# Attention pairs in plain float32: quotients by column halves, one exponential for 512 columns, a reordered weight conversion

## The chip, the cores and the metric

One Trainium2 chip, and of it one core. A core has TensorE (matrix products, PE in the profile, with its weight loads as PEld), VectorE (DVE), ScalarE (ACT), GpSimd (POOL) and SyncE (SP), which issues most DMAs here. Each engine works through its own list of instructions in order and waits on semaphores. The metric is the device time of one execution in microseconds, as the median of several runs.

## The reference

Three stages in a row, all in float32. The attention has 4 batches of 8 heads, 576 positions and 64 columns per head; `omega` is 128 x 64.

```python
def phi(x):                                   # x: q or k, scaled by D ** -0.25
    proj = np.einsum('bhsd,md->bhsm', x, omega)
    h = proj - np.sum(x * x, axis=-1, keepdims=True) / 2.0
    h = h - np.max(h, axis=-1, keepdims=True)
    return np.exp(h) / np.sqrt(m)
kv = np.einsum('bhsm,bhsd->bhmd', k_p, v)
z = np.sum(k_p, axis=2)
num = np.einsum('bhsm,bhmd->bhsd', q_p, kv)
den = np.einsum('bhsm,bhm->bhs', q_p, z)[..., None] + 1e-06
attn = num / den
```

Its result, as 2304 rows of 512 columns, goes through two MLPs with a hidden width of 2048: `h = x @ w_in`, then `max(h, 0) + alpha * min(h, 0)` in the first and 0, `(h + 1) ** 2 / 4` or `h` by ranges in the second, then `g @ w_out`.

## The kernel before

**The attention** goes by pairs of heads: 16 pairs, four for each batch. For a pair, `features` multiplies `omega` with the keys (and later the queries) of both heads, four blocks of 128 positions each, into one PSUM bank per head; `last_features` does the remaining 64 positions. `exponentials` takes each row's maximum on VectorE (`nm`) and then the exponential on ScalarE, one instruction for each block of 128 columns, because the maximum enters as a bias that holds for one block alone. `key_sums` gives `kv` and `z` (a column of ones beside `v`); its copies out of PSUM are `kv_hi`. `transposed` turns the query features (`qh`). `quotients` multiplies `qh` with `kv` and `z`, for half of the positions and one head at a time, into 64 rows of numerators and 64 rows of denominators of one bank; VectorE turns the denominators (`den`), ScalarE or VectorE copies the numerators (`num`). `back` inverts `den` and lets GpSimd multiply both into `x`, the input of the first MLP.

The first six pairs (`N_FULL`) use plain float32 products. The later pairs, and both MLPs, use three products of a faster kind with operands split in two, a rounded part (`_hi`) and the rest (`_lo`): `mm3`. Splitting costs a ScalarE copy and a subtraction, on VectorE for `x`, `g` and the queries, on GpSimd for weights.

**The weights** arrive as float64 bit patterns (`raw`). `convert` makes float32 of each 128 x 512 tile: two scalings (ScalarE, the first one sometimes on GpSimd), a shift and a sign step on VectorE, an addition on GpSimd. Sixteen weight blocks (`f`) of each MLP have two such tiles.

**The MLPs** go by units: for one MLP, one group of positions and one weight block, `hidden` computes `h` from `x` (12 products of 512 columns for a batch), `activate` makes `g`, and `project` adds to four banks `y` (12 more products). The groups are batches 0, 1, 2, and 3 with the left-over positions. So the first unit needs pairs 0 to 3, and pairs 4 to 15 run between the units of the first MLP. The products of unit i+1's `h` stand ahead of unit i's `y`, so that `activate` has time.

**The order** on each engine is written out by a planner in Python (class `Plan`). Work is a set of streams that yield steps with an engine and an assumed duration; the planner repeatedly emits the step that can start first, by rank where several can. Where a step names two engines it takes the one that would end first. The ranks (`attention_rank`, `weight_rank`) say how far ahead of the units attention and weights go. Tokens stand for buffers: `k_slot`, `q_slot`, `l_slot` for the features, `split_slot` for a pair that has not yet all its exponentials, `free_banks` for PSUM banks. The assumed durations are in `_act`, `_dve`, `_pool`, `_dma` and constants as `KV_NS`.

Of the kernel before, what the change touches and what calls it, by code (L numbers as in the profile page):

```python
# [8 lines left out]
F32 = mybir.dt.float32  # L9
# [147 lines left out]
def _dma(nbytes, emit):  # L157
    return "dma", 60 + nbytes / 200, emit
# [3 lines left out]
def favor_attention_two_mlps(  # L162
# [20 lines left out]
    nc = tc.nc  # L183
# [17 lines left out]
    WARM = 18  # L201
    ROWS_NS = 298
# [18 lines left out]
    def attention_rank(pair):  # L221
        b, hp = divmod(pair, NP)
        return hp - 8 if b == 0 else NF * (b - 1) + NF // NP * (hp + 1)
# [43 lines left out]
    def convert(dst, src, key):  # L267

        n = dst.shape[1]
        yield raws  # L270
        raw = stage_p.tile([P, 2 * n], U32, tag="raw", name="raw", bufs=RAWS)
        yield _dma(P * n * 8, lambda: nc.sync.dma_start(raw, src))
        f = raw.bitcast(F32).rearrange("p (n t) -> p n t", t=2)[:, :, 1]
        h = raw.bitcast(U16).rearrange("p (n t) -> p n t", t=4)[:, :, 1]
        low, e = (raw.rearrange("p (n t) -> p n t", t=2)[:, :, t] for t in range(2))
        d = dst.bitcast(U32)

        yield [
            _act(n, lambda: nc.scalar.activation(f, f, AF.Copy, scale=2.0**-112)),
            _pool_one(n, lambda: nc.gpsimd.tensor_scalar(f, f, 2.0**-112, 0.0, ALU.mult, ALU.add), 300),  # L280
        ]
        yield _act(n, lambda: nc.scalar.activation(low, h, AF.Copy, scale=2.0**-13))
        yield _dve_fast(n, lambda: nc.vector.tensor_scalar(d, e, 3, None, ALU.logical_shift_left))  # L283
        yield _pool(n, lambda: nc.gpsimd.tensor_tensor(d, d, low, ALU.add))  # L284
        yield _dve_two(
            n,
            lambda: nc.vector.scalar_tensor_tensor(
                d, e, 0x80000000, d, ALU.bitwise_and, ALU.bitwise_or
            ),
        )  # L290
        plan.put(raws, 0)
        done("w", *key)
# [44 lines left out]
    k_slot, q_slot, l_slot, t_slot, den_slot = (Tokens([0]) for _ in range(5))  # L337
# [9 lines left out]
    def exponentials(pool, pr, tag, dst, key):  # L347
# [6 lines left out]
        yield _dve(n * M, lambda: nc.vector.tensor_reduce(nm, pv, AX.X, ALU.max, negate=True))  # L354
        for i in range(n):
            yield _act(
                M, lambda: nc.scalar.activation(dst[:, i, :], pv[:, i, :], AF.Exp, bias=nm[:, i : i + 1]), 40  # L357
            )
# [3 lines left out]
    def features(pool, x, t0, f, keys, needs, r):  # L362
# [10 lines left out]
        def products():  # L373
            for t in range(NJ):
                c = slice((t0 + t) * P, (t0 + t + 1) * P)
                for h in range(2):
                    rows = slice(h * D, (h + 1) * D)
                    o = prs[h][:, t * M : (t + 1) * M]
                    nc.tensor.matmul(o, x[rows, c], om[rows, h * M : (h + 1) * M], start=True, stop=True)  # L379
# [5 lines left out]
    def last_features(pool, x, lf, key, needs):  # L385
# [5 lines left out]
            432, lambda: nc.tensor.matmul(o, x[:, 2 * NJ * P : 2 * NJ * P + P], om, start=True, stop=True)  # L391
# [3 lines left out]
    def key_sums(pool, kf, lf, vm, vl, pair):  # L395
# [38 lines left out]

        def his():
            for h in range(2):
                o = kv_hi[:, h, cs[h]]
                nc.scalar.activation(o.bitcast(F32) if one else o, kv3[:, h, :D], AF.Copy)
            nc.scalar.activation(z_hi.bitcast(F32) if one else z_hi, z, AF.Copy)
# [7 lines left out]
        yield "act", 370, his  # L447
        if not one:
            yield "dve", 472, los
# [38 lines left out]
    def quotients(kv_hi, kv_lo, qh, ql, den, num, i, h, pair):  # L488
# [3 lines left out]
        if pair < N_FULL:  # L492
            a, b = kv_hi[:, h, :].bitcast(F32), qh[:, h, c].bitcast(F32)
            yield _pe(490, lambda: nc.tensor.matmul(n[:, :SH], a, b, start=True, stop=True))
        else:
            yield _pe(
                mm3_ns(SH),
                lambda: mm3(n[:, :SH], kv_hi[:, h, :], kv_lo[:, h, :], qh[:, h, c], ql[:, h, c], True, True),
            )
        done("n", pair, i, h)  # L500
        own, other = (slice(0, D), slice(D, 2 * D))[:: 1 - 2 * h]

        yield "dve", 508, lambda: nc.vector.transpose(den[own, c], n[other, :SH])
        yield [
            _act(SH, lambda: nc.scalar.copy(num[own, c], n[own, :SH]), 0),
            _dve(SH, lambda: nc.vector.tensor_copy(num[own, c], n[own, :SH]), 50),
        ]
        give(tag)
        done("den", pair, i, h)

    def back(pool, qh, ql, b, hp, pair):
# [6 lines left out]
        num = pool.tile([P, S], F32, tag="num", name="num")  # L518
        for i in range(2):
            for h in range(2):  # L520
                plan.add(quotients(kv_hi, kv_lo, qh, ql, den, num, i, h, pair), attention_rank(pair), pair - 50)
# [55 lines left out]
    def attend(pool):  # L577
        for pair in range(B * NP):
# [3 lines left out]
            yield split_slot  # L582
# [7 lines left out]
            lf = pool.tile([P, 2, M], F32, tag="lf", name="lf")  # L590
# [14 lines left out]
            for key in ("k0", "k1", "l", "q0", "q1"):  # L605
                yield ev(key, pair)
            plan.put(split_slot, 0)
# [216 lines left out]
    om = pool.tile([P, 2 * M], F32, name="om")  # L824
    nc.vector.memset(om, 0.0)
    nc.vector.memset(half, 0.5)

    warm = const.tile([P, 1], F32, name="warm")
    nc.scalar.activation(warm, half, AF.Exp)
    warm_w = const.tile([P, 2 * M], F32R, name="warm_w")  # L830
    nc.vector.memset(warm_w.bitcast(F32), 0.0)
# [3 lines left out]
    for i in range(2):  # L835
        nc.scalar.dma_start(om[i * D : (i + 1) * D, i * M : (i + 1) * M], omega)
# [24 lines left out]
    def constants():  # L861
        make_identity(nc, ident)
        nc.scalar.activation(om, om, AF.Copy, scale=QK_SCALE)

# [65 lines left out]
```

## Time and profile before

| | |
|---|---|
| median of 3 runs | 942.61 us (942.48 to 943.08) |
| the profiled execution | 942.46 us, of which the span of the trace is 940.7 us |
| TensorE | 920.2 us busy, 98% of the span, granted clock 0.999 |
| VectorE, ScalarE, GpSimd | 549.5, 521.5 and 453.7 us busy |

Engines, lines and idle times are named in the rows below. A line number is that of the kernel before. A row of a timeline gives start, duration, engine, line, operation, output and input tiles; in brackets stands the idle time of the engine just before it and what ended it. Durations of instructions that follow each other closely overlap: what one costs its engine is the distance to the next start.

### The profile page before, as it was taken

To read this page: it belongs to the slowest core of one execution; us is meant where nothing else is said; L and a number is where in the kernel's file an instruction comes from. 1 tells how busy PE (TensorE), PEld (TensorE's weight loads), DVE (VectorE), ACT (ScalarE), POOL (GpSimd) and SP (SyncE) were. 2 spreads that over 40 slices of the span, in tenths; PEclk is the share of its full clock that TensorE was granted. 3 is DMA by queue.
4 is the path that set the end of the run, shared out by engine and by line. 5 is a ranking of instruction groups with operands and counts; after the bars stand their busy time and mean duration, and the time that the engine had idled before them with its cause. 6 is when DMAs were issued, how large, how long until landed. Compare 5 with 4: busy or idle time off the path is not lost.

```text
span 940.7 us, 14096 instructions
## 1 busy us (share of the span) xinstructions
PE 920.2 (98%) x5196; PEld 760.6 (81%) x5196; DVE 549.5 (58%) x927; ACT 521.5 (55%) x1120; POOL 453.7 (48%) x374
## 2 busy tenths in 40 slices
PE   8889999999999999999999999999999999999997
PEld 6667887788887888878888888888888888888886
DVE  4898787866667567777764443353335344533332
ACT  6989767655556645655642354464446445543343
POOL 1658776443334357766762344444444444332330
PEclk9999999999999999999999999999999999999999
DMA  7555443111121001334420000010001000100002
GB/s 209 172 157 175 150 150 128 39 38 39 39 63 65 2 1 45 114 111 135 135 91 1 1 0 1 1 45 1 0 1 45 1 1 1 45 1 1 1 1 68
DMA packets 33861, 53.41 MB, mean 57 GB/s; under 512 B 20992, under 2 KB 21120, under 8 KB 33792
## 3 DMA queue, kind: packets, MB, share of 16 engines
q1 hardware_dynamic: 33632, 52.45, 17.4%
q8 instruction: 41, 0.67, 0.3%
q14 instruction: 28, 0.23, 0.1%
q10 hardware_dynamic: 160, 0.07, 0.0%
HBM read 47.78 MB, written 4.72 MB: 56 GB/s over the span
## 4 chain that ended last, share of the span: by engine, by line
PE 89%; DVE 4%; ACT 4%; issue 1%; DMA 0%; POOL 0%; ACTq 0%
PE h L258 14%; PE h L259 14%; PE h L257 14%; PE y L257 12%; PE y L258 12%; PE y L259 12%; PE a L257 2%; PE a L379 2%; PE a L259 2%; PE a L258 2%; ACT kf L357 1%; PE a L416 1%; PE a L464 1%; ACT qf L357 1%; DVE x_lo L251 1%; DVE nm L354 1%
## 5 line engine op out<-in xcount | busy, mean ns | idle before, releaser
L252 POOL TENSOR_TENSOR w_lo<-w,w_hi 128x512 fp32r<-128x512 f32 x256 | 335.7, 1312 | 394.4 <-ACT w_hi L241 387.4
L241 ACT ACTIVATE w_hi<-w 128x512 fp32r<-128x512 f32 x256 | 161.6, 632 | 197.1 <-PE h L258 125.7
L257 PE MATMUL h<-x_hi,w_hi 128*128 128x512 f32 (+1 forms) x640 | 239.9, 375 | 0.0
L258 PE MATMUL h<-x_lo,w_hi 128*128 128x512 f32 (+1 forms) x640 | 236.2, 369 | 2.9 <-DVE x_lo L251 2.9
L259 PE MATMUL h<-x_hi,w_lo 128*128 128x512 f32 (+1 forms) x640 | 236.0, 369 | 0.2 <-POOL w_lo L252 0.2
L241 ACT ACTIVATE g_hi<-h 128x512 fp32r<-128x512 f32 (+1 forms) x160 | 88.9, 555 | 94.0 <-DVE h L679 46.5
L258 PEld LDWEIGHTS h<-x_lo,w_hi 128*128 128x128 f32 x640 | 120.7, 189 | 23.8 <-DVE x_lo L251 4.2
L257 PEld LDWEIGHTS h<-x_hi,w_hi 128*128 128x128 f32 x640 | 120.7, 189 | 21.2 <-DVE g_lo L250 0.8
L259 PEld LDWEIGHTS h<-x_hi,w_lo 128*128 128x128 f32 x640 | 120.6, 188 | 21.0 <-POOL w_lo L252 0.6
L250 DVE TENSOR_TENSOR g_lo<-h,g_hi 128x512 fp32r<-128x512 f32 (+1 forms) x160 | 100.7, 636 | 52.5 <-ACT g_hi L241 50.2
L677 DVE TENSOR_SCALAR t<-h 128x512 f32<-128x512 f32 x80 | 51.0, 638 | 131.3 <-PE h L259 129.6
L284 POOL TENSOR_TENSOR w<-w,raw 128x512 uint32<-128x512 uint32 x64 | 87.1, 1364 | 39.4 <-DVE w L283 23.2
L673 DVE TENSOR_SCALAR t<-h,alpha_sb 128x512 f32<-128x512 f32 x80 | 55.6, 694 | 85.3 <-PE h L259 83.8
L257 PE MATMUL y<-g_hi,w_hi 128*128 128x512 f32 x256 | 104.6, 408 | 0.0
L258 PE MATMUL y<-g_lo,w_hi 128*128 128x512 f32 x256 | 100.3, 392 | 0.0
L259 PE MATMUL y<-g_hi,w_lo 128*128 128x512 f32 x256 | 100.0, 391 | 0.0
L257 PE MATMUL y<-w_hi,g_hi 128*128 128x512 f32 x256 | 99.8, 390 | 0.0
L258 PE MATMUL y<-w_lo,g_hi 128*128 128x512 f32 x256 | 99.8, 390 | 0.0
L259 PE MATMUL y<-w_hi,g_lo 128*128 128x512 f32 x256 | 99.6, 389 | 0.0
L678 ACT ACTIVATE t<-t,half 128x512 f32<-128x512 f32 x80 | 54.5, 681 | 59.9 <-DVE t L677 59.9
L679 DVE TENSOR_TENSOR h<-h,t 128x512 f32<-128x512 f32 x80 | 51.5, 644 | 49.6 <-ACT t L678 49.6
L259 PEld LDWEIGHTS y<-g_hi,w_lo 128*128 128x128 f32 x256 | 48.1, 188 | 10.5
(113 smaller groups left out, 1282.0 us busy)
## 6 DMA issues: line engine op xcount, KB each, us to landing
raw<-w SPq DMA_DIRECT2D x64, 512.0 KB, 4.2
kq<-kq SPq DMA_DIRECT2D x15, 576.0 KB, 4.9
vm<-v SPq DMA_DIRECT2D x16, 256.0 KB, 3.2
out<-x SPq DMA_DIRECT2D x16, 256.0 KB, 2.0
vl<-v SPq DMA_DIRECT2D x32, 16.0 KB, 2.9
out<-x SPq DMA_DIRECT2D x4, 128.0 KB, 2.3
kq<-kq SPq DMA_DIRECT2D x1, 320.0 KB, 4.0
kq<-kq SPq DMA_DIRECT2D x1, 256.0 KB, 2.8
```

Source lines behind the costliest of these rows:

```text
L241: ops = [_act(n, lambda: nc.scalar.activation(hi, src, AF.Copy))]
L250: "dve": _dve(n, lambda: nc.vector.tensor_tensor(*args), bias),
L252: "pool": _pool(n, lambda: nc.gpsimd.tensor_tensor(*args)),
L257: nc.tensor.matmul(out_, wh, mh, start=first, stop=False)
L258: nc.tensor.matmul(out_, wh, ml, start=False, stop=False)
L259: nc.tensor.matmul(out_, wl, mh, start=False, stop=last)
L284: yield _pool(n, lambda: nc.gpsimd.tensor_tensor(d, d, low, ALU.add))
L357: M, lambda: nc.scalar.activation(dst[:, i, :], pv[:, i, :], AF.Exp, bias=nm[:, i : i + 1]), 40
L673: yield _dve(n, lambda: nc.vector.tensor_scalar(tn, hn, 0.0, a, ALU.min, ALU.mult))
L677: yield _dve(n, lambda: nc.vector.tensor_scalar(tn, hn, -1.0, 1.0, ALU.max, ALU.min))
L678: yield _act(n, lambda: nc.scalar.activation(tn, tn, AF.Square, bias=half[:, 0:1], scale=0.5), 50)
L679: yield _dve(n, lambda: nc.vector.tensor_tensor(hn, hn, tn, ALU.max))
```

## The change

It touches the float32 pairs (0 to 5), the conversion of weights and the planner's figures.

1. Quotients of float32 pairs: `full_quotients` takes two banks for half of the positions. One gets the products with `z` of both heads (64 columns of weights each, head 0 into rows 0 to 63, head 1 into rows 64 to 127), the other those with `kv`. Two transposes of 128 rows for a pair take the place of four of 64 rows, and so do two copies of `num`.
2. For the second head of a float32 pair (`k1`, `q1`), VectorE subtracts the maxima of all 512 columns on the way out of PSUM, and one ScalarE exponential takes all 512.
3. The copies of `kv` and `z` of a float32 pair are two in place of three and may go to VectorE.
4. In `convert` the sign step works on the scaled low bits and stands ahead of the shift; GpSimd's addition is last. For the first ten tiles the planner prefers GpSimd for the first scaling.
5. `split_slot` is gone, `l_slot` has two buffers. Attention of batches 1 to 3 has a rank lower by 4. The planner's DMA rate is 340 in place of 200 bytes per ns, and the assumed costs of the key-sum copies of later pairs are higher.
6. `omega` is loaded once per half on two queues (ScalarE's ahead of its table load, SyncE's first of all), 128 columns wide; `om_two` is copied from it.

```diff
-    return "dma", 60 + nbytes / 200, emit
+    return "dma", 60 + nbytes / 340, emit
...
-        return hp - 8 if b == 0 else NF * (b - 1) + NF // NP * (hp + 1)
+        return hp - 8 if b == 0 else NF * (b - 1) + NF // NP * (hp + 1) - 4
...
-            _pool_one(n, lambda: nc.gpsimd.tensor_scalar(f, f, 2.0**-112, 0.0, ALU.mult, ALU.add), 300),
+            _pool_one(n, lambda: nc.gpsimd.tensor_scalar(f, f, 2.0**-112, 0.0, ALU.mult, ALU.add), -600 if early else 300),
...
-        yield _dve_fast(n, lambda: nc.vector.tensor_scalar(d, e, 3, None, ALU.logical_shift_left))
-        yield _pool(n, lambda: nc.gpsimd.tensor_tensor(d, d, low, ALU.add))
+
         yield _dve_two(
             n,
             lambda: nc.vector.scalar_tensor_tensor(
-                d, e, 0x80000000, d, ALU.bitwise_and, ALU.bitwise_or
+                low, e, 0x80000000, low, ALU.bitwise_and, ALU.bitwise_or
             ),
         )
+        yield _dve_fast(n, lambda: nc.vector.tensor_scalar(d, e, 3, None, ALU.logical_shift_left))
+        yield _pool(n, lambda: nc.gpsimd.tensor_tensor(d, d, low, ALU.add))
...
+        if key[0] in ("k1", "q1") and key[1] < N_FULL:
+
+            most = nm.unsqueeze(2).to_broadcast([P, n, M])
+            yield _dve(n * M, lambda: nc.vector.tensor_tensor(dst, pv, most, ALU.add))
+            give(tag)
+            yield _act(n * M, lambda: nc.scalar.activation(dst, dst, AF.Exp), 10)
+            done(*key)
+            return
...
+        def his_dve():
+            kvz = kv_hi.bitcast(F32).rearrange("m a (h d) -> m a h d", h=2)
+            nc.vector.tensor_copy(kvz[:, 0], kv3[:, :, :D])
+            nc.vector.tensor_copy(kvz[:, 1], z)
...
-        yield "act", 370, his
+        yield [("act", 420, his), ("dve", 420, his_dve, -200)] if one else ("act", 590, his)
...
+    def full_quotients(kvz, qt, den, num, i, pair, r):
...
+        def products():
+            for a in (1, 0):
+                for h in range(2):
+                    o = ns[a][h * D : (h + 1) * D, :SH]
+                    nc.tensor.matmul(o, kvz[:, a, h, :], qt[:, h, c], start=True, stop=True)
+
+        yield _pe(COLS_NS, products)
+        done("n", pair, i, 0)
+        done("n", pair, i, 1)
+        plan.add(evicted(turned(den[:, c], ns[1][:, :SH]), tags[1], ("den", pair, i, 1)), *r)
+        plan.add(evicted(copied(num[:, c], ns[0][:, :SH]), tags[0], ("den", pair, i, 0)), *r)
...
-            yield split_slot
...
-            lf = pool.tile([P, 2, M], F32, tag="lf", name="lf")
+            lf = pool.tile([P, 2, M], F32, tag="lf", name="lf", bufs=2)
...
+    for queue, r in ((nc.scalar, slice(0, D)), (nc.sync, slice(D, 2 * D))):
+        queue.dma_start(om[r, :], omega)
...
-    for i in range(2):
-        nc.scalar.dma_start(om[i * D : (i + 1) * D, i * M : (i + 1) * M], omega)
```

How the order moves on TensorE around the first unit's `h`, of before (`h_544` is the first unit's hidden bank, `h_896` the second's; L494 a quotient of pair 4, L410 and L416 the key sums of pair 5):

```order
L494 MATMUL y_841<-qh,kv_hi 128x288
L257 MATMUL h_544<-x_hi,w_hi 128x512
...
L259 MATMUL h_544<-x_hi,w_lo 128x512
L494 MATMUL a_889<-qh,kv_hi 128x288
L494 MATMUL y_903<-qh,kv_hi 128x288
...
L494 MATMUL y_909<-qh,kv_hi 128x288
L410 MATMUL y_917<-vl_122,lf 64x130 x2
L416 MATMUL y_917<-vm_121,kf 64x65 x16
```

And of the change (`h_386` is the first unit's bank; L552 the new quotients of pair 4, L425 and L431 the key sums of pair 5, L489 a transpose of pair 5, L394 and L406 features of pair 6):

```order
L552 MATMUL a_855<-qh,kv_hi 64x288 x2
L425 MATMUL y_870<-vl_123,lf 64x130 x2
L431 MATMUL y_870<-vm_122,kf 64x65 x16
L491 MATMUL a_896<-ident,lf 128x128
L258 MATMUL h_386<-x_hi,w_hi 128x512
L259 MATMUL h_386<-x_lo,w_hi 128x512
L260 MATMUL h_386<-x_hi,w_lo 128x512
L489 MATMUL a_901<-ident,qf 128x128 x4
...
L406 MATMUL y_916<-om_two,kq 128x256
L258 MATMUL h_386<-x_hi,w_hi 128x512
```

All quotients of pair 4 and the key sums of pair 5 now stand ahead of the first `h`; the key and left-over features of pair 6 stand inside it, and the query features of pair 6 and the second transpose of pair 5 follow ahead of the first `y`, where before they stood after it.

On VectorE, between the split of the first input (`x_lo`) and the first step of `activate` (`t`), of before:

```order
L251 TENSOR_TENSOR x_lo<-x_127,x_hi 128x512 x4
L287 SCALAR_TENSOR_TENSOR w<-raw,w 128x512
L283 TENSOR_SCALAR w<-raw 128x512
L503 STREAM_TRANSPOSE den<-y_841 64x288
L673 TENSOR_SCALAR t<-h_544,alpha_sb 128x512
```

And of the change, from the instruction after `x_lo`:

```order
L530 STREAM_TRANSPOSE den<-a_844 128x288
L530 STREAM_TRANSPOSE den<-y_856 128x288
L288 SCALAR_TENSOR_TENSOR raw<-raw 128x512
L589 TENSOR_SCALAR inv<-den 128x18
L590 RECIPROCAL inv<-inv 128x18
L288 SCALAR_TENSOR_TENSOR raw<-raw 128x512
L594 STREAM_TRANSPOSE den<-inv 128x576
L292 TENSOR_SCALAR w<-raw 128x512
L361 TENSOR_REDUCE nm<-y_805 128x4
L361 TENSOR_REDUCE nm<-y_906 128x4
L365 TENSOR_TENSOR qf<-y_805,nm 128x4x128
L728 TENSOR_SCALAR t<-h_386,alpha_sb 128x512
```

Twelve VectorE instructions in place of four now lead from `x_lo` to the first `t`: pair 4's inversion, a query half of pair 5 and the first key maxima of pair 6 are among them.

## Rows read from the trace of the kernel before

**Rows 1.** The page, part 1: busy us, share of the span, instructions.

```profile
PE 920.2 (98%) x5196; PEld 760.6 (81%) x5196; DVE 549.5 (58%) x927; ACT 521.5 (55%) x1120; POOL 453.7 (48%) x374
```

**Rows 2.** Busy time by stretch: PE, PEld, DVE, ACT, POOL, then PEclk, DMA, GB/s.

```profile
20.00:40.00 20.00, 16.31 (x175) 11.59 (x174) 16.48 (x35) 19.85 (x67) 10.60 (x11) 1.00 0.64 201
40.00:60.00 20.00, 16.33 (x175) 12.00 (x176) 18.33 (x33) 19.29 (x58) 11.67 (x11) 1.00 0.55 166
```

**Rows 3.** Timeline of PE: key features of pairs 0, 1, 5; first `h`; first `y`.

```profile
6.46 2.08 PE L379 MATMUL y<-om,kq 64*128 64x128 f32 x16 [0.78 <-ACT om L863]
14.82 1.16 PE L379 MATMUL a<-om,kq 64*128 64x128 f32 x16
...
53.84 1.16 PE L379 MATMUL y<-om,kq 64*128 64x128 f32 x16
...
58.55 0.50 PE L258 MATMUL h<-x_lo,w_hi 128*128 128x512 f32 x1 [0.92 <-DVE x_lo L251]
...
67.00 0.39 PE L257 MATMUL y<-g_hi,w_hi 128*128 128x512 f32 x1
```

**Rows 4.** Timeline of ACT, before the first unit.

```profile
5.99 0.42 ACT L863 ACTIVATE om<-om 128x256 f32<-128x256 f32 x1 [3.76 <-DMA om<-omega]
...
33.68 0.69 ACT L241 ACTIVATE w_hi<-w 128x512 fp32r<-128x512 f32 x1
34.20 0.73 ACT L282 ACTIVATE raw<-raw 128x512 uint32<-128x512 uint16 x1
...
37.87 0.50 ACT L357 ACTIVATE kf<-y,nm 128x128 f32<-128x128 f32 x1
38.12 0.44 ACT L505 COPY num<-y 64x288 f32<-64x288 f32 x1
```

**Rows 5.** Timeline of DVE, before the first unit; then two lines of tile raw, 0:60.

```profile
28.91 1.50 DVE L503 STREAM_TRANSPOSE den<-y 64x288 f32<-64x288 f32 x3
...
40.48 0.29 DVE L480 COPY qh<-a 128x128 f32<-128x128 f32 x1
...
44.59 1.01 DVE L354 TENSOR_REDUCE nm<-y 128x4 f32<-128x512 f32 x2
...
53.26 0.78 DVE L535 STREAM_TRANSPOSE den<-inv 128x576 f32<-128x576 f32 x1
...
L283 DVE TENSOR_SCALAR w<-raw x7: 380/414/1505, 23.0 to 54.5; 128x512 uint32<-128x512 uint32 x7
L287 DVE SCALAR_TENSOR_TENSOR w<-raw,w x6: 649/685/878, 30.4 to 54.0; 128x512 uint32<-128x512 uint32 x6
```

**Rows 6.** Timeline of PE among units: key sums, then a quotient, between MLP products.

```profile
90.21 1.10 PE L416 MATMUL a<-vm,kf 128*64 128x65 f32 x32
91.24 0.50 PE L257 MATMUL y<-g_hi,w_hi 128*128 128x512 f32 x1
91.58 0.40 PE L258 MATMUL y<-g_lo,w_hi 128*128 128x512 f32 x1
91.81 0.40 PE L259 MATMUL y<-g_hi,w_lo 128*128 128x512 f32 x1
92.05 0.65 PE L494 MATMUL a<-qh,kv_hi 128*128 128x288 f32 x2
...
92.76 0.39 PE L258 MATMUL h<-x_lo,w_hi 128*128 128x512 f32 x1
```

**Rows 7.** The chain that ended last: start us, us, what (attention between units).

```profile
73.10 0.44 PE a L464 x4
74.94 1.42 PE a L379 x16
...
80.02 0.48 PE a L391 x2
...
83.92 1.09 PE a L379 x16
```

**Rows 8.** Waits of PE: line, releaser, us in total, times, longest.

```profile
PE a L391 <- ACT kf L357: 2.1, 1, 2.1
```

## What the change does to the time, forecast

> **What bounds the kernel now.** I read the page first: TensorE is busy for 98% of the span [rows 1], so from the first MLP product on the kernel is a queue of products, and time can be won in two ways only, by less TensorE work or by less TensorE idle time. The table of busy time by stretch shows where idle time sits: from 20 to 60 us TensorE is busy 16.3 of every 20 us, while ScalarE has 19.85 and 19.29, and VectorE 16.48 and 18.33 [rows 2]. That front, in which the first pairs run before batch 0 can enter the first MLP, is bound by ScalarE. The timeline of TensorE then gives its rhythm [rows 3]: the key features of pair 0 start at 6.46, those of pair 1 at 14.82, those of pair 5 at 53.84, so a pair takes (53.84 - 14.82) / 4 = 9.76 us. The first product of `h` that has its operands starts at 58.55, the first `y` at 67.00. Behind that `y` TensorE hardly stops, so I take the end as the time of the first `y`, plus TensorE's work behind it, plus later stalls. The sum is made against the profiled execution, 942.46 us; its span is 940.7, and the median of the runs lies 0.15 above it.
>
> **The start.** `om` waits 3.76 us for its DMA and is scaled at 5.99 [rows 4]. Both halves of `omega` now leave at the same time on two queues, ahead of ScalarE's table load and of all else on SyncE, and 128 columns are scaled in place of 256. I take 1.1 us off: the first features at 5.3 in place of 6.46. Bounds: 0, if the landing does not move, and 1.8, half of the wait. The key block that now leaves second on SyncE is hidden behind the same wait. Pair 0 loses its own detour too: `k1`'s features stand right behind the key sums of pair 0, ahead of pair 0's query transposes and quotients. VectorE has pair 0's maxima and subtractions done some 4 us after the first features end (7.4), the key sums follow at about 12, and pair 1's key features end at about 13.2; before they ended at 14.82 + 1.1 = 15.9.
>
> **A pair of the front, on ScalarE.** Starts that follow each other give 0.25 us for an exponential of 128 columns (37.87 to 38.12) and 0.52 for 512 columns (33.68 to 34.20) [rows 4]. Before, a pair has 18 of the first (4.5 us), two and a quarter copies of 512 for `qh` (1.1), four copies of `num` at about 0.3 (1.2), `kv_hi` (0.4) and its share of weight work (2.4 scalings and 0.8 `w_hi`, 1.7): 8.9 of the 9.76. Now it has 10 exponentials of 128 columns (2.5) and two of 512 (1.0), `qh` (1.1), two copies of `num` (0.6), 1.8 scalings and 0.8 `w_hi` (1.4), and no `kv_hi`: 6.6 us. The 512-column exponential is not in the trace; the `w_hi` row bounds it from below (0.52) and that row's full duration, 0.69, from above. A copy of 128 rows I take as one of 64, since a transpose of 576 columns and 128 rows takes 0.78 and three of 288 columns and 64 rows take 1.50 [rows 5]: columns cost, rows do not. If rows did cost, a copy would be at most 0.6.
>
> **The same pair on VectorE.** Two maxima, one of 512 and one of 256 columns, take 1.01 together [rows 5], so 0.61 and 0.34 with about 0.06 between. Before: four maxima of 512 and one of 256 (2.8), four transposes (2.0), inversion with the 0.78 transpose (1.2), shift and sign steps (1.2 of each at 0.38 to 0.41 and 0.65 to 0.69: 1.3), stray copies 0.4: 7.7 us. Now two transposes less (-1.0), two subtractions of 512 columns more, two copies of `kv` more, no stray copies. The subtraction is new: it reads PSUM and writes SBUF for 512 columns, as many elements as a maximum reads, so 0.61; the slowest row of 512 columns here, the sign step, has 0.878 at most. I take 0.61. The `kv` copies are 128 columns as the 0.29 row, about 0.21 each in sequence. Sum: 7.7 - 1.0 - 0.4 + 1.2 + 0.4 = 7.9 us. The sign step now writes every second word; I leave it at 0.65, with 0.878 as the upper end.
>
> **TensorE in that pair.** A quotient between MLP products takes 92.76 - 92.05 - 0.23 = 0.48 us [rows 6]. Key sums use the same column halves as the new quotients: 32 passes of 65 columns take 91.24 - 90.21 = 1.03, or 0.064 for two passes; a full quotient's 0.48 for 288 columns makes 0.24 a pass, that is 0.054 for 65 columns, so two passes there run side by side. Four half-width products then take two times 0.48 = 0.96, plus the change of form: the product behind the key sums starts 0.34 after its predecessor in place of 0.23, and I count 0.1 on either side, 1.16 for half a pair in place of 0.96. In the front that lies under VectorE: 1.2 + 1.2 + 0.5 of features, 1.3 of key sums, 1.1 of transposes, 2.3 of quotients are 7.6 us, still below 7.9. The page "TensorEngine Tiling (Array Packing)" of the Trainium skill, Tiling Modes, Key Properties, says that a change of tiling mode drains the engine, which speaks against mixing such quotients into MLP products; the trace agrees with about 0.1 us for each change, and without it the sum would be 0.4 us lower for pair 5, the one pair that runs among units.
>
> **The rhythm.** So VectorE takes over as the bound with 7.9 us. ScalarE reached its 9.76 with 8.9 of work, 91%; I give VectorE the same, 7.9 / 0.91 = 8.7 us for a pair. Pair 5's key features end at 13.2 + 4 x 8.7 = 48.0, where before they ended at 54.9. The DMAs cover this: three weight tiles are now issued ahead of pair 2's keys, 1.6 MB, at 201 GB/s [rows 2] some 8 us from about 7, and those keys (0.6 MB, 3 us) are issued at about 12 and needed at about 21. Without that cover it would cost once what they come late.
>
> **From there to the first `y`.** The order on VectorE says what stands between pair 5's key features and the first `t`: two maxima of 512, one of 256, a subtraction, another maximum, three `x_hi` at about 0.41 and four `x_lo` at 0.62 (6.5 us), then the twelve rows shown, 5.7 us. With the same 91% that is 13.4, so `t` starts at 61.4 + 0.2 for the first hop. Two steps of `activate`, two maxima and a shift between them, ScalarE's `g_hi` and `g_lo` add 3.7: the first `y` can start at 65.3. TensorE gets there earlier (about 15 us of work from 48.0), so VectorE decides. Against 67.00 that is 1.7 us.
>
> **Work that is no longer behind it.** Ahead of the first `y` now stand two query transposes, the key, left-over and query features of the next pair. Their pieces in the chain of before are 0.44 (twice), 1.42, 0.48 and 1.09 [rows 7]: 3.9 us. Against it pair 5's quotients grow from 4 x 0.48 to 2 x 1.16, 0.4 us. Net 3.5.
>
> **Sum.** 1.7 + 3.5 = 5.2 us: 942.46 - 5.2 = 937.3 for a profiled run, 937.4 as a median. Behind the first `y` the loads are alike: the later attention pairs are the same work four units earlier, and I leave the later stalls as they are. The steps of the weight conversion are the same in number; one hop between engines goes, and nothing waits on it now. Cost zero, covered by TensorE's queue of products.
>
> **Rivals.**
> The front gets no shorter. VectorE at 0.88 for each subtraction and sign step has 8.7 us a pair, at 91% 9.6, and the rhythm stays. Pair 5 then ends at 13.2 + 38.4 = 51.6 and the first `y` comes at 69 or 70; of the 5.2 us stay about 1, so 941.2. For it: VectorE already has 18.33 of 20 us [rows 2], and its shift has once taken 1505 ns in place of 414 [rows 5]. GpSimd now has four scalings more in the front with which that can happen. The page "SBUF — State Buffer" of the Trainium skill, SBUF: two separate sides, calls the pair of ports that the two engines share an exclusive lock; by that each collision costs up to a whole GpSimd instruction, and the trace agrees with 1.1 us for the one shift that met one. Against it: the new subtraction reads PSUM, as the maxima do, and those hold their 0.61.
>
> Slower: stalls among the units. Attention of batches 1 to 3 goes four units earlier, into the phase in which weights are still converted. There TensorE once stood 2.1 us because features waited for a bank that ScalarE had not emptied [rows 8]; in-order, all products wait behind it. Three pairs (6, 7, 8) now run there. If each brings one or two such stalls, four in all, 8.4 us are lost: 937.4 + 8.4 = 945.8. It decides from about 7.1 us of new stalls on. For it: VectorE and GpSimd carry the same work in this phase plus a pair. Against it: the planner has these waits in its account, and TensorE gets more work there as well.
>
> The column halves do not run side by side: 1.92 + 0.2 for half a pair. TensorE then has 9.5 us a pair, the front keeps its rhythm and pair 5 loses 2.3 us: about 942.5, no change. The key sums speak against it.
>
> Better: VectorE without gaps, 7.9 us a pair, and 12.2 in place of 13.4 afterwards: pair 5 ends at 44.8, the first `y` at 61.0, 6.0 + 3.5 = 9.5 us, 933.0.
>
> **Chances.** My forecast 0.55 (its own range 935 to 940.5), better 0.14, no shorter front 0.16, stalls 0.12, no side by side 0.03. What a measurement can tell is 0.2%, 1.9 us. Faster than 940.7: the forecast, the better case and a third of the unshortened front, 0.73. Slower than 944.5: most of the stalls, 0.11. Same: 0.16. The range from 932.5 to 942.8 leaves out part of the better case and most of the stalls.
>
> **What would show it.** Key features of pair 5 ending near 48 and those of pair 1 near 13; VectorE, no longer ScalarE, near 18 to 19 of 20 us in the front; the first `y` near 65; the subtraction at about 0.69 and its successor 0.61 later; half a pair's quotients within 1.2 us; TensorE's idle time from 140 to 180 us no longer than before. I am wrong if pairs still take 9.7 us, or if waits on ScalarE or VectorE behind 70 us add up to several microseconds more than now.

## The result, and the profile after

The changed kernel takes 930.61 us in the median of four runs (929.68 to 931.66), beside 942.85 for the kernel before: ratio 0.9876, 95% interval 0.9864 to 0.9887. The forecast, 937.4 with a range down to 932.5, had the sign and less than half of the size. The profiled execution took 930.48 us, 11.98 less than that of before; its span is 928.7. Of e5, below, one execution took 2347 us, the profiled one; it is left out of the median, and e5 has no rows.

Part 1 of the page (busy us, share of the span, instructions), beside [rows 1]:

```profile
PE 914.9 (99%) x5244; PEld 759.3 (82%) x5244; DVE 543.0 (58%) x942; ACT 508.4 (55%) x1052; POOL 456.0 (49%) x375
```

Busy time by stretch after, columns as in [rows 2]; the first two rows answer to it, the next three are the units:

```profile
20.00:40.00 20.00, 18.67 (x235) 14.36 (x236) 18.67 (x40) 18.03 (x50) 15.72 (x16) 1.00 0.67 198
40.00:60.00 20.00, 18.14 (x191) 13.78 (x188) 18.83 (x40) 14.94 (x44) 9.50 (x11) 1.00 0.60 181
60.00:140.00 80.00, 79.32 (x525) 62.96 (x524) 64.56 (x121) 60.04 (x145) 52.94 (x44) 1.00 0.47 152
140.00:182.00 42.00, 40.46 (x275) 32.04 (x273) 34.76 (x62) 30.51 (x77) 28.61 (x22) 1.00 0.31 93
182.00:450.00 268.00, 267.79 (x1557) 222.70 (x1556) 186.47 (x323) 156.70 (x342) 149.59 (x118) 1.00 0.21 70
```

And of before, two of the stretches that were not shown:

```profile
140.00:182.00 42.00, 38.86 (x265) 30.13 (x264) 33.76 (x59) 29.01 (x77) 26.06 (x21) 1.00 0.28 87
182.00:450.00 268.00, 266.21 (x1590) 219.09 (x1589) 183.26 (x313) 154.30 (x355) 138.65 (x115) 1.00 0.19 60
```

ScalarE went from 19.85 and 19.29 to 18.03 and 14.94 us, VectorE from 16.48 to 18.67. TensorE is now as busy as VectorE (18.67 of 20 us from 20 to 40); that VectorE is the bound of the front, as forecast, rests on e9 below. Behind the first `y`, TensorE's idle time fell from 4.96 to 2.45 us (summed over the gaps between its records; the rows show 3.14 and 1.79 before, 0.68, 1.54 and 0.21 after).

TensorE's timeline after, beside [rows 3]: features of pair 0, of pair 1's and of pair 5's keys, first `y`:

```profile
5.33 1.57 PE L394 MATMUL y<-om,kq 64*128 64x128 f32 x16
...
11.15 0.37 PE L394 MATMUL y<-om,kq 64*128 64x128 f32 x1
...
43.81 0.48 PE L394 MATMUL y<-om,kq 64*128 64x128 f32 x2
45.28 0.37 PE L394 MATMUL a<-om,kq 64*128 64x128 f32 x1 [0.98 <-ACT num L534]
...
62.05 0.50 PE L258 MATMUL y<-g_hi,w_hi 128*128 128x512 f32 x1
```

The 11.98 us are therefore: 4.95 by the earlier first `y` (67.00 to 62.05), 2.5 by less idle time behind it, and the remainder, 4.5, by TensorE's busy time that is no longer behind it.

The new operations, on VectorE for pair 2, and then the split of the first input (beside [rows 5]):

```profile
22.74 0.68 DVE L365 TENSOR_TENSOR kf<-y,nm 128x512 f32<-128x512 f32 x1
23.34 0.68 DVE L361 TENSOR_REDUCE nm<-y 128x4 f32<-128x512 f32 x1
...
25.47 0.83 DVE L530 STREAM_TRANSPOSE den<-y 128x288 f32<-128x288 f32 x2
...
49.18 1.09 DVE L244 CAST x_hi<-x 128x512 fp32r<-128x512 f32 x3
50.19 2.49 DVE L252 TENSOR_TENSOR x_lo<-x,x_hi 128x512 fp32r<-128x512 f32 x4
```

on ScalarE (beside [rows 4]), `om` and then a 512-column exponential with its successor:

```profile
3.15 0.31 ACT L919 ACTIVATE om<-om 128x128 f32<-128x128 f32 x1 [0.33 <-DMA om<-omega]
...
48.80 0.66 ACT L367 ACTIVATE kf<-kf 128x512 f32<-128x512 f32 x1
49.32 0.66 ACT L242 ACTIVATE x_hi<-x 128x512 fp32r<-128x512 f32 x1
```

and on TensorE the two halves of a pair's quotients, from 23.57 to the next product at 25.65:

```profile
23.57 0.70 PE L552 MATMUL y<-qh,kv_hi 128*64 128x288 f32 x3
24.07 0.69 PE L552 MATMUL a<-qh,kv_hi 128*64 128x288 f32 x4
24.57 1.19 PE L552 MATMUL y<-qh,kv_hi 128*64 128x288 f32 x8
25.65 0.44 PE L425 MATMUL a<-vl,lf 128*64 128x130 f32 x4
```

The subtraction costs 0.60 to the next start, the exponential 0.52, half a pair's quotients 1.04, two transposes of 128 rows no more than two of 64 did. These operations came at the prices that the forecast gave them.

### The profile page after: what moved, and what is told of

Read it like the earlier page. It is cut to its first block, busy times and chain, and to the rows that moved or that the text cites. A ratio compares the mean times of both kernels' runs of the same rounds, so it can differ in the third digit from the quotient of the medians.

```text
span 928.7 us, 14192 instructions
## 1 busy us (share of the span) xinstructions
PE 914.9 (99%) x5244; PEld 759.3 (82%) x5244; DVE 543.0 (58%) x942; ACT 508.4 (55%) x1052; POOL 456.0 (49%) x375
## 4 chain that ended last, share of the span: by engine, by line
PE 89%; DVE 5%; ACT 2%; DMA 1%; SPq 1%; issue 1%; POOL 0%; ACTq 0%; DVEq 0%
PE h L258 14%; PE h L260 13%; PE h L259 13%; PE y L258 12%; PE y L259 12%; PE y L260 12%; PE a L258 2%; PE a L260 2%; PE a L259 2%; PE a L394 2%; DMA raw<-w 1%; DVE x_lo L252 1%; PE a L431 1%; PE a L489 1%; DVE nm L361 1%
## 5 line engine op out<-in xcount | busy, mean ns | idle before, releaser
L253 POOL TENSOR_TENSOR w_lo<-w,w_hi 128x512 fp32r<-128x512 f32 x256 | 336.6, 1316 | 387.8 <-ACT w_hi L242 382.0
```

The source lines that it names most:

```text
L253: "pool": _pool(n, lambda: nc.gpsimd.tensor_tensor(*args)),
```

## The experiments

"First y" and "idle" (TensorE's idle time behind the first `y`) are from each profiled execution. How much attention stands ahead of the first `y` differs between orders, so a late first `y` is no loss by itself.

| kernel | median us | first y | idle |
|---|---|---|---|
| before | 942.85 | 67.0 | 5.0 |
| changed | 930.61 | 62.1 | 2.5 |
| e1 points 1 to 3 alone | 937.9 | 60.6 | 5.6 |
| e2 point 5 alone | 946.8 | 74.0 | 6.7 |
| e3 point 6 alone | 941.9 | 66.1 | 4.9 |
| e4 point 4 alone | 937.6 | 65.8 | 1.7 |
| e5 point 4, steps only | 947.3 | | |
| e6 point 4, scalings only | 945.3 | 74.5 | 6.5 |
| e7 changed without point 4 | 938.2 | 66.7 | 5.6 |
| e8 changed without point 5 | 941.7 | 66.3 | 5.4 |
| e9 subtraction twice | 937.6 | 69.8 | 2.4 |
| e10 figure of the exponential | 941.0 | 62.6 | 10.8 |
| e11 figure of the quotients | 935.0 | 64.1 | 4.8 |
| e12 old rank | 937.3 | 65.9 | 7.4 |
| e13 new steps, old order | 955.2 | 70.0 | 11.0 |
| e14 `kv` copies on ScalarE | 930.6 | 61.2 | 3.7 |
| e15 a quarter of the subtraction | 930.5 | 60.8 | 2.2 |
| e16 figure of the features | 935.9 | 68.2 | 7.0 |
| e17 figure of the key sums | 941.1 | 62.2 | 10.4 |
| e18 rank one earlier | 935.7 | 75.5 | 2.4 |

**Each part alone (e1 to e4)**: the kernel before with the lines of the points named, of which one or two stand here.

```diff
 e1, points 1 to 3
+        if key[0] in ("k1", "q1") and key[1] < N_FULL:
...
+            if pair < N_FULL:
+                plan.add(full_quotients(kvz, qh.bitcast(F32), den, num, i, pair, r), *r)
 e2, point 5
+    return "dma", 60 + nbytes / 340, emit
...
-            yield split_slot
 e3, point 6
+        queue.dma_start(om[r, :], omega)
 e4, point 4
+                low, e, 0x80000000, low, ALU.bitwise_and, ALU.bitwise_or
```

> The kernel before with points 1 to 3 of the change alone (quotients by column halves, one exponential of 512 columns, kv copies where the planner likes); start, weight conversion and the planner's figures as before. Theory A: the rhythm of the front is what was won, because ScalarE's work for a pair falls from 8.9 to about 6.6 us; then a pair takes 8.3 to 8.8 us in place of 9.76 and the kernel about 936 us. Theory B: most was won by the planner's figures and the freed buffers; then this kernel stays at 940 or above.

> The kernel before with point 5 alone (no split slot, two buffers for the left-over features, rank lower by 4, DMA rate 340, the two key-sum costs). Theory A: the front stays bound by ScalarE and keeps 9.7 us a pair; 941 to 943.5 us. Theory B: 937 to 939, with less idle TensorE time from 140 to 410 us.

> The kernel before with point 6 alone (omega loaded by halves on two queues). Theory A: in a front bound by ScalarE an earlier start passes through one to one: first features at 5.3 in place of 6.46, so 941.2 to 941.8 us. Theory B: it is lost in later waits, 942.3 to 943.

> The kernel before with point 4 alone (sign step ahead of the shift, GpSimd preferred for the first scaling of ten tiles). Theory A: ScalarE loses about four scalings of 0.56 us in the front, so 940.5 to 941.5 us. Theory B: the addition on GpSimd at the end of each conversion delays weights; 942.8 or slower.

e1 reaches about theory A. Its key features of pair 1 and of pair 5 start at

```profile
13.74 0.37 PE L393 MATMUL a<-om,kq 64*128 64x128 f32 x1
...
46.67 0.37 PE L393 MATMUL y<-om,kq 64*128 64x128 f32 x1
```

so points 1 to 3 by themselves bring a pair from 9.76 to 8.23 us. e2 and e4 came out outside both of their expectations, and e3 between its two.

Ratios to before: e1 0.9953 (0.9938 to 0.9968), e2 1.0044 (1.0031 to 1.0057), e3 0.9997 (0.9988 to 1.0007), e4 0.9955 (0.994 to 0.997). The conversion, which I had priced at nothing, gives as much as the products. The four together make -6.1 us by their medians (942.58 for before beside them), the whole -12: the parts do not add.

**Point 4 cut in two (e5, e6)**, on the kernel before:

```diff
 e5
-                d, e, 0x80000000, d, ALU.bitwise_and, ALU.bitwise_or
+                low, e, 0x80000000, low, ALU.bitwise_and, ALU.bitwise_or
...
+        yield _dve_fast(n, lambda: nc.vector.tensor_scalar(d, e, 3, None, ALU.logical_shift_left))
+        yield _pool(n, lambda: nc.gpsimd.tensor_tensor(d, d, low, ALU.add))
 e6
-    ..., ALU.mult, ALU.add), 300),
+    ..., ALU.mult, ALU.add), -600 if early else 300),
```

> The kernel before, with the sign step of a weight conversion moved ahead of the shift and put into the low bits; the choice of engine for the first scalings stays. Theory (steps): the conversion now ends on GpSimd's addition, with one crossing between engines less, so w_hi waits shorter at the head of ScalarE's queue and the exponentials behind it free their banks in time: the 3.3 us of TensorE stalls between 140 and 450 us go, about 939 us, first y no earlier than 67. Rival (engine of the first scalings): the gain of 5 us came from ScalarE's lighter start, and this kernel stays within 1 us of 942.6.

> The kernel before, with GpSimd preferred for the scalings of batch 0's first weights alone; order of the conversion's steps as before. Theory (steps): only the front can change, by the 1.2 us that the first y came earlier with both halves of the edit: 941.4 us, with the stall of 2 us at 142 us still there. Rival (engine of the first scalings): 938 us and the stalls gone.

All four expectations fell: 947.31 (ratio 1.0062, 1.0044 to 1.008) and 945.27 (1.004, 1.0024 to 1.0056). Either half costs time, and both together gain 5 us.

**Parts taken out of the whole (e7, e8, e12)**: the changed kernel with the old `convert`; with the old figures of point 5; with the old rank alone.

```diff
 e7
-                low, e, 0x80000000, low, ALU.bitwise_and, ALU.bitwise_or
+                d, e, 0x80000000, d, ALU.bitwise_and, ALU.bitwise_or
...
 e8, and in it e12 (the rank alone)
-    return "dma", 60 + nbytes / 340, emit
+    return "dma", 60 + nbytes / 200, emit
...
+            yield split_slot
...
-        return hp - 8 if b == 0 else NF * (b - 1) + NF // NP * (hp + 1) - 4
+        return hp - 8 if b == 0 else NF * (b - 1) + NF // NP * (hp + 1)
```

> The changed kernel with the old weight conversion (order of steps and choice of engine). If the 5 us that the conversion gave alone stand by themselves: 930.6 + 5 = 935.6 us, of it about 1.2 in the first y and the rest in stalls behind it. Rival (the shorter front alone has done away with the stalls, by another order of the work): within 1.5 us of 930.6.

> The changed kernel with the planner's old figures (cost of a DMA, the four units' earlier rank, the second slot of the left-over features and the slot for one pair at a time). Alone on the kernel before these figures cost 4.2 us. If they cost that here too: 926.4 us, a version faster than both. Rival (the figures need the lighter front and give here what the parts' sum lacks: -12 in all against -6 for the sum of the four parts alone): 933 to 937 us, with attention of the first pairs back among the products behind the first y.

> The changed kernel with the attention of batches 1 to 3 at its old rank, four units later; all else as changed. The old figures together cost 8 to 11 us there. Theory (the figures as such matter little, any change of order costs as much): 934 to 938 us, the first y within 1 us of 62.05, more idle time of TensorE from 60 to 450 us. Rival (the four units are what empties the later phase of stalls): 938 us or more; by the prediction's own rival, that earlier attention brings stalls, it would fall below 930.

Medians 938.17, 941.73, 937.29. Without the conversion the changed kernel loses 7.6 us, where I expected 5 or nothing. The figures, a loss of 4 us alone, are worth 11 here; e8 is outside both of its expectations too. With the old rank it loses 6.7, and the idle time is 7.4 us, not less: my rival that earlier attention would bring stalls did not come true here. But all three losses are of the size that any other order brings (below, 4 to 10 us), so they do not tell what the conversion, the figures or the rank is worth by itself. The first `y` of e12, forecast within 1 us of 62.05, came at 65.9.

**Is VectorE the bound? (e9, e15, e14)** All three keep the changed kernel's order on every engine. (In e14, ten instructions move and not twelve: ScalarE had one pair's copies already.)

```diff
 e9:  +  for _ in range(2):  nc.vector.tensor_tensor(dst, pv, most, ALU.add)
 e15: +  nc.vector.tensor_tensor(part, pv[:, :, :32], most[:, :, :32], ALU.add)
...
 e14: -  ("dve", 420, his_dve, -200)
      +  ("dve", 420, his, -200)        # planned for VectorE, issued on ScalarE
```

> The changed kernel, every engine's order of work untouched, with each of the 12 subtractions of 512 columns done twice; nothing else differs. Theory (VectorE bounds the front, as predicted, only with less work or less idle time than I counted): each repeat costs its 0.60 us, less what its gaps of 1.2 of 20 us take in; 12 x 0.60 = 7.2, so 935.5 to 938 us. Rival (TensorE, busy 18.67 of 20 us in the same stretch, now bounds the front): below 933.5 us.

> The changed kernel, order kept, with each of the 12 subtractions done for 32 of each 128 columns (128 of 512) and the exponential taken over these columns four times; it leaves out three quarters of the subtraction. About 0.4 us less on VectorE each time, 4.8 us in all. If VectorE alone bounds the front: first y 4 to 4.8 us earlier, 926 us. Rival (TensorE, 18.67 of 20 us busy, is next at once): 1 to 2 us, about 929.

> The changed kernel, order of work kept, with the copies of kv done by ScalarE at the very places where VectorE did them: 12 instructions, 2 a pair at 0.15 to 0.20 us each, off VectorE. If VectorE bounds every stretch of the front: first y 2 us earlier, 928.5 us, faster than both kernels. Rival (ScalarE, at 18.03 of 20 us from 20 to 40, hands the delay back): within 0.7 us of 930.6.

e9: 937.6 us; the first `y` came at 69.78, 7.73 later for 7.2 us of VectorE, and the idle time behind it stayed. Busy time by stretch of e9:

```profile
20.00:40.00 20.00, 16.44 (x229) 12.67 (x223) 19.53 (x44) 16.03 (x45) 11.49 (x12) 1.00 0.54 156
```

VectorE's share rises, TensorE and ScalarE fall back: the theory holds. To the other side it ends soon. In e15 the subtraction takes 0.28 us, 0.8 us less for a pair, yet a pair takes 8.05 us in place of 8.17; in e14 the copies are gone from VectorE. The first `y` came only 1.25 and 0.86 us earlier, as the rivals had it, and the medians are those of the changed kernel (930.54, 930.56; e15's rival had 929). So VectorE is ahead of the next engine by about a microsecond in the whole front; whether that is TensorE (18.67 of 20 us) or ScalarE, e15 and e14 do not tell apart. No version came out faster than the changed kernel.

**The same instructions in other orders (e10, e11, e16 to e18)**

```diff
 e10: -  AF.Exp), 10)         e11: -  COLS_NS = 1260     e16: -  ROWS_NS = 298
      +  AF.Exp), 40)              +  COLS_NS = 1080          +  ROWS_NS = 290
 e17: -  KV_NS = 1480         e18: -  ... * (hp + 1) - 4
      +  KV_NS = 1400              +  ... * (hp + 1) - 5
```

> The changed kernel with one planner figure altered, and no instruction more or less: the 512-column exponential costed 30 ns higher (40 as for the short ones, in place of 10). It measures what a mere change of order is worth. Theory (much of what the prediction missed behind the first y is where the planner's order happens to put the waits): the time moves by several microseconds, to 933 to 938 us, in TensorE's idle time from 60 to 450 us. Rival (the order is robust and the stalls went for a reason of the change): within 1 us of 930.6.

> The changed kernel with one planner figure altered, no instruction more or less: half a pair's quotients costed at 1080 ns, as the trace has them (1.0 to 1.08 us), in place of 1260. Theory (order scatters): several microseconds from 930.6, either way, and not the same as with the figure for the exponential. Rival (robust): within 1 us; a truer figure might even win a little.

> The changed kernel with the planner's cost of a piece of features at 290 in place of 298 ns; same instructions. Theory (the changed kernel's order is an exceptional one): 934 to 941 us, nearly all of it idle time of TensorE behind the first y. Rival (the two orders measured were unlucky): within 1.5 us of 930.6, or below it, a faster version.

> The changed kernel with the planner's cost of a pair's key sums at 1400 in place of 1480 ns; same instructions. Theory (exceptional order): 934 to 941 us. Rival (the two orders measured were unlucky): within 1.5 us of 930.6, or below.

> The changed kernel with the attention of batches 1 to 3 one more unit earlier (rank -5 in place of -4); same instructions, and an unchanged front. Theory (exceptional order): 933 to 940 us, with the first y where it is and more idle time behind it. Rival: within 1.5 us of 930.6, or below; if each unit earlier helped, as four of them seem to, 929.

Medians 940.97, 934.97, 935.92, 941.09, 935.68: a number in the planner costs 4 to 10 us with no instruction more or less (the planner sends 4 to 13 of those that may go to two engines to the other one). e10 and e17 are above the ranges of their theories. With e8 and e12 that makes seven other orders of the changed kernel's instructions, from 934.97 to 941.73, median 937.29. The order of the changed kernel is 4.4 us better than the best of them. e18 did not keep its front: two groups of features more than in the changed kernel went ahead of its first `y`, and the idle time behind that is no longer than in the changed kernel. Counted from the first features to the last product, TensorE was idle for 13.2 us before, 7.6 in the changed kernel and 10.1 (e18) to 15.9 (e10) in the seven. To that comes TensorE's clock (last section): in their profiled executions e8, e10 and e12 lose up to 1.7 us at its lower level, e17 and e18 up to 3.4; before and the changed kernel lose none.

What such an order does is seen in e10. Waits of TensorE from 62 to 450 us, the longest of e10, then all of the changed kernel's between 60 and 450:

```profile
PE a L491 <- DVE ql L251: 4.1, 1, 4.1
PE a L258 <- ACT num L534: 2.4, 2, 1.8
```

```profile
PE a L425 <- ACT qf L372: 1.1, 2, 0.7
PE a L394 <- ACT lf L372: 0.9, 1, 0.9
PE h L260 <- POOL w_lo L253: 0.2, 1, 0.2
PE a L258 <- ACT num L534: 0.2, 1, 0.2
```

VectorE's timeline of e10 ahead of that wait:

```profile
174.24 4.04 DVE L252 TENSOR_TENSOR x_lo<-x,x_hi 128x512 fp32r<-128x512 f32 x3
178.21 1.48 DVE L244 CAST x_hi<-x 128x512 fp32r<-128x512 f32 x1
179.70 0.75 DVE L728 TENSOR_SCALAR t<-h,alpha_sb 128x512 f32<-128x512 f32 x1
180.37 0.68 DVE L251 TENSOR_TENSOR ql<-a,qh 128x512 fp32r<-128x512 f32 x1
```

GpSimd's `w_lo` of e10 in the same stretch (ns: min/median/max, first and last start):

```profile
L253 POOL TENSOR_TENSOR w_lo<-w,w_hi x2: 1702/1714/1726, 176.0 to 177.7; 128x512 fp32r<-128x512 f32 x2
```

In this order VectorE's split of `x` stands ahead of the `ql` for which TensorE waits, and it runs beside GpSimd: three `x_lo` took 4.04 us and the `x_hi` 1.48, where the rows of the changed kernel's front show 2.49 for four and 1.09 for three. TensorE works in order, so all products behind it wait. e17 has the same 4.1 us. That the collision makes these stalls is read from the trace; it was not tested by itself.

**New steps in the old order (e13)**: the kernel before, nothing replanned.

```diff
-        yield _dve_fast(n, lambda: nc.vector.tensor_scalar(d, e, 3, None, ...))
+        yield _dve_fast(n, signs_and_shift)      # sign step into low, then the shift
         yield _pool(n, lambda: nc.gpsimd.tensor_tensor(d, d, low, ALU.add))
-        yield _dve_two(n, ...)                   # the sign step
+        yield _dve_two(n, lambda: None)
```

> The kernel before, its order of work kept on every engine, with the new conversion's steps in it: sign step (into the low bits) and shift one after the other at the shift's old place, GpSimd's addition last. If the steps as such end the stalls (conversion ready one crossing earlier, w_hi no longer at the head of ScalarE's queue): TensorE's 2.08 us stall at 144 us and most of the others go, about 939 us. Rival (the planner's order did it): within 1.5 us of 942.5, idle time behind the first y still 4 to 6 us.

955.24 us (ratio 1.0135, 1.0118 to 1.0151): both fell. The steps by themselves do not end the stalls; in an order made for others they cost 12 us, 7.8 of them in the profile as idle time of TensorE. The shift on VectorE from 60 to 450 us (count, busy, mean ns, idle before it), of before:

```profile
L283 DVE TENSOR_SCALAR w<-raw 128x512 uint32<-128x512 uint32 x46 | 27.8, 622 | 0.9 <-ACT raw L279 0.9
```

the same of e13:

```profile
L285 DVE TENSOR_SCALAR w<-raw 128x512 uint32<-128x512 uint32 x43 | 35.9, 834 | 0.0
```

and a wait of VectorE in e13 (us in total, times, longest):

```profile
DVE raw L284 <- ACT raw L282: 2.7, 3, 1.4
```

The shift right behind the sign step is slower by a third, and the sign step now waits for ScalarE's scaled low bits in VectorE's queue. That these two make the idle time was not tested.

## Why the forecast had the direction and not the size

- **The start**: right in the number, by luck. 1.1 us were forecast, 6.46 to 5.33 is 1.13. But `om` is scaled at 3.15 in place of 5.99, 2.8 us earlier, beyond my bound of 1.8, and no longer decides: TensorE is still at its warm-up products, and the features follow these without a wait.
- **The operations' prices** (0.69 with the successor 0.61 later, 0.52 to 0.69, 1.16 or less, columns cost and rows do not): right, see the rows above. The column halves run side by side, since a pair's quotients take 2.08 us and not 3.8. That the 0.1 us on either side belongs to the change of form is not shown: in the kernel before, a product behind transposes, which keep the form 128*128, also starts its successor 0.31 later:

```profile
72.94 0.60 PE L464 MATMUL a<-ident,qf 128*128 128x128 f32 x4
73.30 0.48 PE L257 MATMUL y<-g_hi,w_hi 128*128 128x512 f32 x1
73.61 0.40 PE L258 MATMUL y<-g_lo,w_hi 128*128 128x512 f32 x1
```

- **VectorE takes over as the bound**: right, shown by e9, but it is barely ahead of the next engine (e14, e15).
- **The rhythm**: wrong in size. The step that failed is "I give VectorE the same, 7.9 / 0.91 = 8.7 us for a pair". A pair measured (43.81 - 11.15) / 4 = 8.17. Both of its terms were off. The 91% was no share of busy time: it set a count of ScalarE's work, 8.9, against 9.76, while ScalarE was in fact busy for 37.02 of 39.02 us, 95%. And VectorE's work is 30.41 / 4 = 7.60 us a pair and not 7.9, at 93%. Pair 1's features came at 11.15 + 1.2 = 12.3 in place of 13.2. From pair 5's first maximum at 46.26 to the first `t` at 57.96 it took 11.7 us, where "with the same 91% that is 13.4" had 12.2 of work; it was 11.60. The stretch of [rows 3] before, and then these two after (columns as in [rows 2]):

```profile
14.82:53.84 39.02, 32.56 (x350) 23.16 (x349) 32.51 (x63) 37.02 (x120) 18.98 (x18) 1.00 0.59 176
11.15:43.81 32.66, 30.02 (x388) 22.70 (x384) 30.41 (x68) 29.26 (x79) 19.13 (x20) 1.00 0.77 238
46.26:57.96 11.70, 11.14 (x113) 8.48 (x112) 11.60 (x24) 8.05 (x24) 5.43 (x7) 1.00 0.54 167
```

  Together this is the first `y` at 62.05 in place of 65.3: 3.2 us of the 6.8 that were missed. The rhythm does not hang on the order: e10 has 8.20 (features at 11.66 and 44.45).
- **The rivals**: the unshortened front and the slow column halves fell by the same rows. The better case had the first `y` at 61.0, a microsecond from what came, and nothing on the stalls either. Stalls among the units did not come in the changed kernel; in other orders of its work they did (7.0 to 10.8 us of idle time in e10, e12, e16 and e17, against 5.0 before), but not because of the earlier rank, since e12 has them without it.
- **Work no longer behind the first `y`**: the pieces were the right ones (TensorE has 288 products of features behind it in place of 320, 90 transposes in place of 98), the sizes not. By the distances between the records behind the first `y`, features and transposes are 3.6 us less (forecast 3.9) and quotients 1.1 more (forecast 0.4). The other 2.0 of the 4.5 I did not have: the MLP's products stand closer, in part because 90 in place of 100 of them come right behind an attention product, where one takes 0.24 to 0.37 in place of 0.23.
- **"I leave the later stalls as they are" and "Cost zero, covered by TensorE's queue of products"**: these failed as well, with 2.5 us here, and e10 shows 8 the other way. I took the order behind the first `y` as given because the work is alike. The planner orders anew whatever changes, and the new order decides which in-order queue has a long step ahead of what TensorE needs. That the stall of [rows 8] went in the changed kernel for that reason is the likeliest reading: e4, with the conversion alone, has 1.7 us of idle time, e6 with half of the edit 6.5, e13 with the steps in the old order 11.0, e10, with all steps of the changed kernel, 10.8.

That my 937.4 lies beside the median of the seven other orders, 937.29, is luck: it left out 3 us in the front, and those orders lose 4 to 11 us in idle time and clock, which it did not have either. Why the changed kernel's order is the best of the eight, the runs do not tell. Whether the figures of point 5 have a merit beyond the order that they lead to stays open: alone they cost 4 us, in the whole they are worth 11, and other figures near them cost 4 to 10.

## What to carry to other kernels

Where a planner writes the order, any edit is two edits: what the instructions cost, which rows of the trace tell, and a new order, which here moved the time by 4 to 10 us with the same instructions; so keep the order fixed when an edit is to be judged, take the spread from a few idle changes of figures, and put that spread into the range. Parts of such a change cannot be added up from runs of each part alone. And when one engine hands the bound to another, take the new rhythm from the new engine's own work and from how close the next engines follow, and take a share of busy time from the trace, not from a count of work.

## What the runs showed of the hardware

A stall can cost more than itself. Behind e10's stall of 4.06 us the granted clock was 0.57 in the mean of the next 4 us, most of them at the lower of its two levels, 1.2 in place of 2.4 GHz, and products stood 0.43 us apart in place of 0.23:

```profile
176.74 0.39 PE L260 MATMUL y<-g_hi,w_lo 128*128 128x512 f32 x1
181.19 0.30 PE L491 MATMUL a<-ident,lf 128*128 128x128 f32 x1 [4.06 <-DVE ql L251]
...
182.06 0.63 PE L260 MATMUL h<-x_hi,w_lo 128*128 128x512 f32 x1
182.49 0.63 PE L258 MATMUL h<-x_hi,w_hi 128*128 128x512 f32 x1
```

```profile
181.00:185.00 4.00, 3.81 (x11) 3.04 (x12) 2.64 (x6) 0.77 (x2) 0.00 (x0) 0.57 0.00 0
```

The length of a stall alone does not decide this. Behind the stall of 2.08 us of before it stayed at 1.00; e3 has nearly the order of before and the same stall, 2.05 us long, and behind it the clock was 0.51 (first before, then e3):

```profile
144.20:148.00 3.80, 3.80 (x27) 3.00 (x28) 1.07 (x3) 2.18 (x6) 3.80 (x4) 1.00 0.54 197
143.90:147.30 3.40, 3.40 (x15) 2.39 (x15) 0.42 (x1) 1.86 (x4) 3.39 (x4) 0.51 0.49 183
```

The ten executions of e3 differ by this: with a mean clock of 0.999 one took 939.96 us, with 0.997 five took 941.37 to 942.05, with 0.995 four took 943.19 to 943.47. So the 1.1 us that point 6 gives at the start is not to be seen in e3's median.

And VectorE and GpSimd slow each other when both work between SBUF tiles: `x_lo` and `w_lo` of 512 columns took 1.7 us each while they ran side by side in e10, where each alone takes some 0.68 and 1.3 (`w_lo` has a mean of 1316 ns over the changed kernel). In the changed kernel the 15 `x_lo` of 512 columns that met no GpSimd instruction took 0.68 us each, the 13 that met one for more than half of their time 1.27 in the median. `g_lo`, the same operation with one input in PSUM, shows nothing of it, though GpSimd worked beside many of them (ns: min/median/max, first and last start):

```profile
L252 DVE TENSOR_TENSOR x_lo<-x,x_hi x40: 405/678/1779, 50.2 to 787.4; 128x512 fp32r<-128x512 f32 x32, 128x256 fp32r<-128x256 f32 x8
L251 DVE TENSOR_TENSOR g_lo<-h,g_hi x160: 411/691/694, 60.6 to 918.5; 128x512 fp32r<-128x512 f32 x128, 128x256 fp32r<-128x256 f32 x32
```
